# Linear attention feeding a gated MLP on one core: the planned order of work kept on every engine, and softmax denominators by a fused multiply-and-add

## The chip, the core and the metric

The kernel runs on one core of a Trainium2 chip. The core has a matrix engine (PE in the profile, with its weight loads as PEld), a vector engine (DVE), a scalar engine for activations and copies (ACT), a general engine (POOL) and SP, which here only issues DMAs. Each engine works through its own queue in the order in which the program stands; an instruction that waits for another engine holds everything behind it on its own engine. The metric is the device time of one execution in microseconds (us). Before the change it is 1099.16 us, the median of three runs (1097.7 to 1101.51).

## The reference

```python
def _attn_ref(q, k, v, omega):            # q, k, v: 8 x 8 x 576 x 64; omega: 128 x 64
    scale = 1.0 / np.sqrt(np.sqrt(D))
    def phi(x):
        proj = np.einsum('bhsd,md->bhsm', x, omega)
        sq = np.sum(x * x, axis=-1, keepdims=True) / 2.0
        h = proj - sq
        h = h - np.max(h, axis=-1, keepdims=True)
        return np.exp(h) / np.sqrt(m)
    q_p, k_p = (phi(q * scale), phi(k * scale))
    kv = np.einsum('bhsm,bhsd->bhmd', k_p, v)
    z = np.sum(k_p, axis=2)
    num = np.einsum('bhsm,bhmd->bhsd', q_p, kv)
    den = np.einsum('bhsm,bhm->bhs', q_p, z)[..., None] + 1e-06
    return num / den

def _moe_ref(x, w_in, w_out):             # x: 4608 x 512; w_in: 512 x 2048; w_out: 2048 x 512
    h = x @ w_in
    return (h * (1.0 / (1.0 + np.exp(-h)))) @ w_out
```

The attention output, with heads side by side, is the x of the MLP. The weights arrive as 64-bit floats.

## The kernel before, in words

**Tiling.** The attention is done for 32 pairs of heads, numbered n: four pairs give the 512 features of one batch t = n // 4, and 576 tokens of two heads make nine chunks of 128 rows (the middle chunk holds the end of one head and the start of the other). The MLP is done in steps (t, f): 512 tokens of batch t against 128 of the 2048 hidden features, 16 steps per batch; the 64 tokens that remain of each batch are kept aside and form a ninth round. Every 32-bit product of the MLP is made of three matmuls on high and low parts, so a step is 12 matmuls into the hidden tile (L495) and 12 into the output tile (L513), each 512 columns wide.

**One pair.** SP loads `raw` (transposed q or k, L238), `nat` (the same by rows, L242) and `v` (L246). ACT squares `nat` (L250), DVE sums the squares (L254). PE projects (L262, L269), DVE takes row maxima (L278, L276) and makes the exponent's shift `nb` (L282, L283), ACT takes the exponential (L298; from pair 8 on L312, after DVE has added the shift). POOL sums the chunks of k (L318 to L323), PE spreads that sum over all partitions (`zsum`, L327) and ACT copies it out (`zcopy`, L335 and L336: tile `zb`). DVE multiplies q's exponentials with `zb` (`products`, L362), sums each chunk (`denom`, L369) and takes reciprocals (L370). POOL multiplies q by them (`normal`, L375), PE transposes the result (`turn`, L381) and ACT copies it (L385). PE makes kv (L343), turns it (L351) and multiplies (`numer`, L399). ACT and DVE split the result into x high and low (L413, L418); that is the MLP's input for feature block k = n % 4.

**Weights.** In the first batch each of the 16 steps also prepares its weights: SP loads a block of w_in and one of w_out (L435, three buffers `wraw` for both), ACT and DVE put 32-bit words together (L442, L456, L458, L462), POOL splits them into high and low (L476, L480). The parts of w_in stay on chip; those of w_out go out to memory (L483) and come back for every step (L487). A hidden tile goes through two activations on ACT (L500, L501) and a subtraction on DVE (L505) before its second matmuls, which come two steps later. The exponential and this activation use different function tables; a change of function costs an ACT_TABLE_LOAD row.

**What sets the order.** All work is cut into units with an engine, a duration, a due time, what they follow and what they need free. `Plan.run` walks time forward with these numbers and returns one list of units. The program emits them in that list's order. In the version before, the framework's own scheduler then sorts the emitted instructions once more by its own estimate of when each could run, so an engine's queue holds them in an order that differs from the list's.

Of the kernel before, what the change touches and what calls it, by code (L numbers as in the profile page):

```python
# [63 lines left out]
class Plan:  # L64
# [6 lines left out]
    def add(self, name, eng, dur, key, fn, after=(), order=(), alloc=(), free=(), banks=0, table=None, lat=0.0):  # L71
        u = dict(
            name=name, eng=eng, dur=dur, key=key, fn=fn, after=list(after), order=list(order), alloc=list(alloc),
            banks=banks, table=table, lat=lat,
        )
        assert name not in self.units, name
        self.units[name] = u
        for i in free:
            self.freed_by.setdefault(i, []).append(name)
# [118 lines left out]
def attention_mlp(ctx: ExitStack, tc: tile.TileContext, qT, kT, qn, kn, v, om_in, w_in, w_out, out):  # L198
# [10 lines left out]
    def new(tag, shape, dtype=F32):  # L209
        return ring.tile(shape, dtype, tag=tag, name=tag, bufs=RINGS[tag])  # L210
# [6 lines left out]
    oms = const.tile([P, M], F32, tag="oms", name="oms")  # L217
    prod = const.tile([P, NC, M + 1], F32, tag="prod", name="prod")
    nc.gpsimd.memset(prod, GUARD)

# [136 lines left out]

    def products(n):
        e, zb = T["h", n, "q"], T.pop(("zb", n))
        for j, (lo, hi) in enumerate(((0, 4), (4, 5), (5, 9))):  # L360
            c = slice(lo, hi)
            nc.vector.tensor_tensor(  # L362
                prod[:, c, :M], e[:, c], zb[:, j].unsqueeze(1).broadcast_to([P, hi - lo, M]), ALU.mult
            )

    def denom(n):
        den = new("den", [P, NC])
        T["rd", n] = rd = new("rd", [P, NC])
        nc.vector.tensor_reduce(den, prod, AX.X, ALU.add)  # L369
        nc.vector.reciprocal(rd, den)  # L370
# [177 lines left out]
    for n in range(NWIN):  # L548
# [67 lines left out]
        if not merged:  # L616
# [7 lines left out]
            alloc=[("kw", ("kw", n))], free=[bk(("ktt", n))])  # L624
        add(("prod", n), "DVE", 1.7, at(n, 8, 34.2), lambda n=n: products(n),
            after=e["q"] + [("zc", n)], order=[("den", n - 1)] if n else [], free=[("zb", n)])
        add(("den", n), "DVE", 1.6, at(n, 8.1, 34.4), lambda n=n: denom(n), after=[("prod", n)],
            alloc=[("den", ("den", n)), ("rd", ("rd", n))])
        plan.freed_by[("den", n)] = [("den", n)]
# [59 lines left out]
    for i, (t, f) in enumerate(steps):  # L689
# [16 lines left out]
        for j in range(4):  # L706
# [11 lines left out]
            if f == NF - 1:  # L718
                add(("store", t, j), "ACT", 0.62, k2 + 0.2, lambda t=t, j=j: store(t, j), after=[("s2", t, f, j)],
                    free=[("po", t, j)])  # L720
    for u in plan.run():
        u["fn"](*[bank(p) for p in u["pools"]])

# [50 lines left out]
```

## Time and profile before

| what | value |
|---|---|
| runs, median (lowest to highest) | 1099.16 us (1097.7 to 1101.51) |
| the profiled execution's own time | 1101.4 us |
| its span, first to last instruction | 1099.3 us |
| mean granted PE clock | 0.976 |
| PE busy, share of the span | 96% |
| DVE / ACT / POOL busy, share of the span | 52% / 53% / 23% |

The profile is of one execution. "Busy" is the time in which an engine had at least one instruction at work; a group row gives the engine, the operation, out and in tiles, the count, the busy time with the mean of one instruction, and then the idle time ahead of them with what ended it. A timeline row gives the start in us, the length in us, and in square brackets how long the engine had been idle and who released it.

### The profile page before, as it was taken

The page shows a single profiled execution, that of the slowest core. Times are in us where ns is not written, and L with a number is a line of the kernel's source. Part 1 is how long each engine was busy: PE and PEld are TensorE (multiplying, and loading weights), DVE is VectorE, ACT ScalarE, POOL GpSimd, SP SyncE. Part 2 cuts the span into 40 slices and gives each one's busy share as a digit, 9 for nine tenths or more (in the row PEclk, how much of TensorE's full clock was granted, in tenths as well). Part 3 has the DMA queues.
Part 4 walks back from the last instruction along what each step waited for, and adds up shares of the span by engine and source line. Part 5 has one row for each costly group of instructions (what it writes and reads, how often), then busy time and mean ns, then how long its engine had stood idle before and what let it go on. Part 6 is the DMA issues. An engine that isn't in the chain of part 4 may idle for free.

```text
span 1099.3 us, 16192 instructions
## 1 busy us (share of the span) xinstructions
PE 1053.1 (96%) x5900; PEld 834.5 (76%) x5900; DVE 566.4 (52%) x1109; ACT 583.1 (53%) x1085; POOL 255.5 (23%) x327
## 2 busy tenths in 40 slices
PE   5677998899999999999999999999999999999998
PEld 4455776687877778777778777787877788888886
DVE  6788897745555455545555455555554431111111
ACT  5557878565556555555556555655565442222211
POOL 3666665411111111111111111111111110000000
PEclk7688999999999999999999999999999999999999
DMA  7576787553335443444345433533343226223323
GB/s 282 198 221 234 265 290 252 182 167 125 124 126 178 139 133 119 136 165 138 122 139 178 140 127 130 173 131 126 123 154 104 80 80 213 96 96 122 109 96 96
DMA packets 66526, 167.84 MB, mean 153 GB/s; under 512 B 15632, under 2 KB 15760, under 8 KB 66448
## 3 DMA queue, kind: packets, MB, share of 16 engines
q1 hardware_dynamic: 65984, 166.23, 45.6%
q8 instruction: 47, 0.77, 0.3%
q10 hardware_dynamic: 464, 0.59, 0.1%
q14 instruction: 31, 0.25, 0.1%
HBM read 146.87 MB, written 19.92 MB: 152 GB/s over the span
## 4 chain that ended last, share of the span: by engine, by line
PE 86%; DVE 5%; DMA 3%; ACT 3%; POOL 1%; issue 1%; SPq 0%; ACTq 0%; DVEq 0%; POOLq 0%
PE ps_acc L513 35%; PE ps_h L495 34%; PE ps_att L262 5%; PE ps_att L343 3%; PE ps_att L381 3%; PE ps_att L399 2%; DMA wraw<-w_out 1%; DMA nat<-qn 1%; PE ps_att L327 1%; PE ps_att L269 1%; DVE w L458 1%; ACT hq L298 1%; DVE w L462 1%; POOL hq L375 1%; DVE den L369 1%
## 5 line engine op out<-in xcount | busy, mean ns | idle before, releaser
L513 PE MATMUL ps_acc<-wo,gh 128*128 128x512 f32 x1152 | 369.9, 402 | 0.0
L500 ACT ACTIVATE gh<-ps_h 128x512 fp32r<-128x512 f32 x144 | 86.2, 599 | 295.9 <-PE ps_h L495 295.3
L505 DVE TENSOR_TENSOR gl<-ps_h,gh 128x512 fp32r<-128x512 f32 x144 | 99.1, 688 | 275.8 <-ACT ps_h L501 275.8
L513 PEld LDWEIGHTS ps_acc<-wo,gh 128*128 128x128 f32 x1152 | 207.1, 189 | 43.7
L495 PE MATMUL ps_h<-xh,wh 128*128 128x512 f32 x576 | 235.0, 409 | 0.3 <-ACT xh L413 0.3
L495 PE MATMUL ps_h<-xh,wl 128*128 128x512 f32 x576 | 226.7, 394 | 0.0
L495 PE MATMUL ps_h<-xl,wh 128*128 128x512 f32 x576 | 225.9, 392 | 0.0
L513 PE MATMUL ps_acc<-wo,gl 128*128 128x512 f32 x576 | 225.8, 392 | 0.0
L375 POOL TENSOR_TENSOR hq<-hq,rd 128x384 f32<-128x384 f32 x96 | 81.7, 879 | 421.4 <-DVE rd L370 396.5
L495 PEld LDWEIGHTS ps_h<-xh,wh 128*128 128x128 f32 x576 | 108.1, 188 | 24.7 <-issue 0.8
L513 PEld LDWEIGHTS ps_acc<-wo,gl 128*128 128x128 f32 x576 | 108.1, 188 | 24.2 <-issue 0.8
L495 PEld LDWEIGHTS ps_h<-xh,wl 128*128 128x128 f32 x576 | 108.1, 188 | 24.1
L495 PEld LDWEIGHTS ps_h<-xl,wh 128*128 128x128 f32 x576 | 108.5, 188 | 22.3 <-DVE xl L418 0.4
L312 ACT ACT_TABLE_LOAD x48 | 61.6, 1283 | 69.2 <-DVE hq L303 53.3
L318 POOL TENSOR_TENSOR t<-hk 128x256 f32<-128x256 f32 x64 | 48.8, 780 | 183.2 <-ACT hk L312 170.1
L278 DVE TENSOR_REDUCE mxq<-ps_att 128x4 f32<-128x512 f32 x57 | 37.2, 687 | 99.7 <-PE ps_att L262 99.6
L501 ACT ACTIVATE ps_h<-ps_h 128x512 f32<-128x512 f32 x144 | 85.3, 593 | 0.0
L500 ACT ACT_TABLE_LOAD x56 | 71.8, 1283 | 22.0 <-PE ps_h L495 21.3
L362 DVE TENSOR_TENSOR prod<-hq,zb 128x512 f32<-128x512 f32 (+1 forms) x96 | 52.3, 595 | 49.6 <-ACT zb L336 47.7
L250 ACT ACTIVATE nat<-nat 128x576 f32<-128x576 f32 x64 | 44.6, 703 | 20.3 <-DMA nat<-kn 12.3
L381 PE MATMUL ps_att<-ident,hq 128*128 128x128 f32 x261 | 41.1, 284 | 7.9 <-POOL wp L476 2.4
L278 DVE TENSOR_REDUCE mxk<-ps_att 128x4 f32<-128x512 f32 x55 | 35.6, 686 | 18.7 <-PE ps_att L262 18.7
(121 smaller groups left out, 1232.0 us busy)
## 6 DMA issues: line engine op xcount, KB each, us to landing
wo<-wo_d SPq DMA_DIRECT2D x144, 512.0 KB, 3.3
rawk<-kT SPq DMA_DIRECT2D x32, 352.0 KB, 3.0
rawq<-qT SPq DMA_DIRECT2D x32, 352.0 KB, 3.8
v<-v SPq DMA_DIRECT2D x32, 320.0 KB, 2.9
nat<-kn SPq DMA_DIRECT2D x32, 288.0 KB, 3.3
nat<-qn SPq DMA_DIRECT2D x32, 288.0 KB, 3.2
wraw<-w_in SPq DMA_DIRECT2D x16, 512.0 KB, 4.6
wraw<-w_out SPq DMA_DIRECT2D x16, 512.0 KB, 4.3
```

What stands on the lines that cost most here:

```text
L262: nc.tensor.matmul(ps[:, i * M : (i + 1) * M], raw[r, o : o + P], oms[r], start=True, stop=True)
L278: nc.vector.tensor_reduce(m[:, 5 * j : 5 * j + 4], ps.rearrange("p (c m) -> p c m", m=M), AX.X, ALU.max)
L312: nc.scalar.activation(h, h, AF.Exp)
L318: nc.gpsimd.tensor_tensor(t[:, j], e[:, 5 * j : 5 * j + 2], e[:, 5 * j + 2 : 5 * j + 4], ALU.add)
L362: nc.vector.tensor_tensor(prod[:, c, :M], e[:, c], zb[:, j].unsqueeze(1).broadcast_to([P, hi - lo, M]), ALU.mult)
L375: nc.gpsimd.tensor_tensor(e[:, c], e[:, c], rd[:, c].unsqueeze(2).broadcast_to([P, 3, M]), ALU.mult)
L381: nc.tensor.transpose(ps[:, i * P : (i + 1) * P], T["h", n, "q"][:, 3 * g + i], ident)
L495: nc.tensor.matmul(ph, w[:, k, :], x, start=k == 0 and n == 0, stop=k == NK - 1 and n == 2)
L500: nc.scalar.activation(gh, ph, AF.Silu)
L501: nc.scalar.activation(ph, ph, AF.Silu)
L505: nc.vector.tensor_tensor(gl, T["ph", t, f], T["gh", t, f].bitcast(F32), ALU.subtract)
L513: nc.tensor.matmul(T["po", t][j], g[:, js], w, start=f == 0 and n == 0, stop=f == NF - 1 and n == 2)
```

## The change

Two things change. The units are emitted inside a block that keeps the emitted order on every engine, so the list of `Plan.run` is what each queue holds. And the denominators are made by nine instructions, one per chunk, that multiply and accumulate in one go, instead of three products into `prod` and one wide sum over it. The guard against division by zero, which before lay in an extra column of `prod` (set once at the start), is now the start value of each accumulation. In the plan the units `prod` (1.7) and `den` (1.6) become one unit `den` with the duration 2.3; since the plan places all others around it, other units stand elsewhere in the list too.

```diff
-    prod = const.tile([P, NC, M + 1], F32, tag="prod", name="prod")
-    nc.gpsimd.memset(prod, GUARD)
+    prod = const.tile([P, NC, M], F32, tag="prod", name="prod")
...
-    def products(n):
+    def denom(n):
         e, zb = T["h", n, "q"], T.pop(("zb", n))
-        for j, (lo, hi) in enumerate(((0, 4), (4, 5), (5, 9))):
-            c = slice(lo, hi)
-            nc.vector.tensor_tensor(
-                prod[:, c, :M], e[:, c], zb[:, j].unsqueeze(1).broadcast_to([P, hi - lo, M]), ALU.mult
+        den = new("den", [P, NC])
+        for c in range(NC):
+            j = (c >= MID) + (c > MID)
+            nc.vector.tensor_tensor_reduce(
+                out=prod[:, c], in0=e[:, c], in1=zb[:, j], scale=1.0, scalar=GUARD, op0=ALU.mult, op1=ALU.add,
+                accum_out=den[:, c : c + 1],
             )
-
-    def denom(n):
-        den = new("den", [P, NC])
         T["rd", n] = rd = new("rd", [P, NC])
-        nc.vector.tensor_reduce(den, prod, AX.X, ALU.add)
         nc.vector.reciprocal(rd, den)
...
-        add(("prod", n), "DVE", 1.7, at(n, 8, 34.2), lambda n=n: products(n),
-            after=e["q"] + [("zc", n)], order=[("den", n - 1)] if n else [], free=[("zb", n)])
-        add(("den", n), "DVE", 1.6, at(n, 8.1, 34.4), lambda n=n: denom(n), after=[("prod", n)],
-            alloc=[("den", ("den", n)), ("rd", ("rd", n))])
+        add(("den", n), "DVE", 2.3, at(n, 8, 34.2), lambda n=n: denom(n), after=e["q"] + [("zc", n)],
+            order=[("den", n - 1)] if n else [], alloc=[("den", ("den", n)), ("rd", ("rd", n))], free=[("zb", n)])
...
-    for u in plan.run():
-        u["fn"](*[bank(p) for p in u["pools"]])
+    with tc.manual_schedule():
+        for u in plan.run():
+            u["fn"](*[bank(p) for p in u["pools"]])
```

Where instructions stand now, at three places. Line numbers of the changed kernel are one to three lower than those of the one before for the same code (L381 is L378, L343 is L342, L399 is L396, L458 is L455, L369 and L370 become L362 and L367, L435 is L432, L423 is L420).

**PE, end of pair 0.** The queue just behind the transposes of pair 0 (`hq`); `es` is the sum that POOL makes for pair 1, `hk,v` the kv product of pair 1, `en,kw` the result of pair 0. Before:

```order
L381 MATMUL ps_h<-ident,hq 128x128 x3
L381 MATMUL ps_att<-ident,hq 128x128 x6
L327 MATMUL ps_h<-es,ones 128x256
L343 MATMUL ps_att<-hk,v 64x128 x10
L399 MATMUL ps_acc<-en,kw 64x512 x2
L399 MATMUL ps_att<-en,kw 64x64 x2
```

And in the changed kernel:

```order
L378 MATMUL ps_h<-ident,hq 128x128 x3
L378 MATMUL ps_att<-ident,hq 128x128 x6
L342 MATMUL ps_att<-hk,v 64x128 x10
L396 MATMUL ps_acc<-en,kw 64x512 x2
L396 MATMUL ps_att<-en,kw 64x64 x2
L326 MATMUL ps_acc<-es,ones 128x256
```

The matmul that waits for POOL's sum of pair 1 has moved from in front of pair 1's kv and pair 0's result to behind both.

**DVE, the denominators of pair 3.** `w_914` is the weight word of step 4's w_in block, `sqq` and `sqk` on L254 and L253 are the sums of squares of later pairs. Before (left out: the other two products and two rows of other pairs ahead of the sum, and two more such rows behind it):

```order
L282 TENSOR_TENSOR nbq<-mxq,sqq 128x9
L458 SCALAR_TENSOR_TENSOR w_914<-wre,w_914 128x512
L283 SCALAR_TENSOR_TENSOR nbq<-nbq,sqq 128x9
L282 TENSOR_TENSOR nbk<-mxk,sqk 128x1
L462 SCALAR_TENSOR_TENSOR w_914<-wraw,w_914 128x512
L283 SCALAR_TENSOR_TENSOR nbk<-nbk,sqk 128x1
L254 TENSOR_REDUCE sqq<-nat 128x9
L278 TENSOR_REDUCE mxq<-ps_att 128x4 x2
L362 TENSOR_TENSOR prod<-hq,zb 128x4x128
...
L369 TENSOR_REDUCE den<-prod 128x9
...
L370 RECIPROCAL rd<-den 128x9
```

And in the changed kernel, where `w_914` stands behind the reciprocal (left out: seven more pairs of such rows as the two on L362):

```order
L281 TENSOR_TENSOR nbq<-mxq,sqq 128x9
L282 SCALAR_TENSOR_TENSOR nbq<-nbq,sqq 128x9
L455 SCALAR_TENSOR_TENSOR w_585<-wre,w_585 128x512
L253 TENSOR_REDUCE sqk<-nat 128x9
L459 SCALAR_TENSOR_TENSOR w_585<-wraw,w_585 128x512
L453 TENSOR_SCALAR w_783<-wraw 128x512
L362 ISA prod,den<-hq,zb 128x128
L362 ISA den 128x1
...
L362 ISA prod,den<-hq,zb 128x128
L362 ISA den 128x1
L367 RECIPROCAL rd<-den 128x9
```

Each multiply-and-accumulate is two instructions in the queue, the second of which writes the one accumulated column; nothing of another unit stands between the first and the reciprocal, and twelve units that stood in front of pair 3's denominators before stand behind them now.

**SP, loads around the weights of steps 6 and 7.** `wraw<-w_in` is a weight block; the two `rest` rows keep aside the tokens of pair 4 and wait for that pair's x; `rawq` waits for a buffer that pair 5's middle projection frees. Before (the first row is the block of step 7):

```order
L435 DMA wraw_1101<-w_in 128x512
L483 DMA wo_d_94<-wp_1133 128x1024
L487 DMA wo_1156<-wo_d_94 128x1024
L435 DMA wraw_1175<-w_out 128x512
L238 DMA rawq_1194<-qT 128x704
L242 DMA nat_1210<-qn 128x576
L487 DMA wo_1217<-wo_d_94 128x1024
L435 DMA wraw_1234<-w_in 128x512
L483 DMA wo_d_94<-wp_1232 128x1024
L246 DMA v_1279<-v 128x640
L423 DMA rest00_86<-xh0_1260 128x64
L423 DMA rest10_90<-xl0_1261 128x64
```

And in the changed kernel (the third row is the block of step 6, the last that of step 7):

```order
L237 DMA rawq_1143<-qT 128x704
L484 DMA wo_1153<-wo_d_93 128x1024
L432 DMA wraw_1200<-w_in 128x512
L432 DMA wraw_1203<-w_out 128x512
L245 DMA v_1215<-v 128x640
L241 DMA nat_1225<-kn 128x576
L480 DMA wo_d_93<-wp_1206 128x1024
L420 DMA rest00_85<-xh0_1190 128x64
L420 DMA rest10_89<-xl0_1191 128x64
L484 DMA wo_1317<-wo_d_93 128x1024
L432 DMA wraw_1323<-w_in 128x512
```

The load of step 7's w_in stood ahead of `rest` of pair 4 and of pair 7's `rawq`, and stands behind both now; that of step 6 stands behind that `rawq`.

On PE, all rows that start after 228 us of the profiled execution stand in the order before, but for 15 of 1,256 units, each moved by one or two places. ACT holds 120 function-table loads before and 112 now; all eight that are gone stood before that point.

## The prediction

> **What bounds the kernel now.** I read the page's head first, then a table of busy time in three stretches that I cut where PE's load changes; its columns are the stretch and its length, then busy time of PE, PEld, DVE, ACT and POOL, the granted PE clock, the DMA share and GB/s.
>
> ```profile
> span 1099.3 us, 16192 instructions
> PE 1053.1 (96%) x5900; PEld 834.5 (76%) x5900; DVE 566.4 (52%) x1109; ACT 583.1 (53%) x1085; POOL 255.5 (23%) x327
> 0.00:25.00 25.00, 13.83 (x108) 11.50 (x108) 15.11 (x35) 13.36 (x39) 6.42 (x14) 0.79 0.79 285
> 25.00:105.00 80.00, 57.94 (x338) 38.98 (x338) 66.53 (x115) 51.28 (x149) 55.03 (x60) 0.74 0.66 211
> 105.00:228.00 123.00, 114.73 (x636) 87.46 (x637) 97.94 (x166) 91.58 (x173) 68.30 (x70) 1.00 0.70 240
> 228.00:1075.00 847.00, 846.79 (x4736) 680.56 (x4735) 383.01 (x788) 422.09 (x716) 125.79 (x184) 1.00 0.40 132
> ```
>
> From 228 to 1075 us PE is idle for 0.2 us in 847, and the order there is nearly the old one: nothing that other engines do can shorten or, short of large delays, lengthen it. PE is idle for 11.2 us up to 25, 22.1 us from 25 to 105 and 8.3 us from 105 to 228. The question is when PE reaches the work that stood at 228. Up to 105 it waits for the attention of the first four pairs; there DVE is the fullest of the others (66.5 of 80 us), and from 105 on PE itself is at 93% with DVE at 80%.
>
> **The multiply-and-accumulate.** Groups of the old denominators, and DVE rows that start close behind each other:
>
> ```profile
> L362 DVE TENSOR_TENSOR prod<-hq,zb 128x512 f32<-128x512 f32 x64 | 47.0, 734 | 49.6 <-ACT zb L336 47.7 <-ACT hq L312 1.9
> L362 DVE TENSOR_TENSOR prod<-hq,zb 128x128 f32<-128x128 f32 x32 | 10.2, 318 | 0.0
> L369 DVE TENSOR_REDUCE den<-prod 128x9 f32<-128x1161 f32 x32 | 43.6, 1362 | 0.9
> 76.78 0.16 DVE L283 SCALAR_TENSOR_TENSOR nbq<-nbq,sqq 128x9 f32<-128x9 f32 x1
> 76.86 0.14 DVE L282 TENSOR_TENSOR nbk<-mxk,sqk 128x1 f32<-128x1 f32 x1
> 76.93 0.68 DVE L462 SCALAR_TENSOR_TENSOR w<-wraw,w 128x512 uint32<-128x512 uint32 x1
> 191.45 0.28 DVE L362 TENSOR_TENSOR prod<-hq,zb 128x128 f32<-128x128 f32 x1
> ```
>
> The rows from 76.78 on start 0.08 and 0.07 apart though each lasts longer, so successive instructions overlap by some 0.08. Old: 2 x 0.734 + 0.318 + 1.362, less 4 x 0.08, is 2.83 us a pair. New: no row shows the instruction. Low end: the undisturbed 128-column product of the last row less overlap, 0.20, and 0.07 for the one-column write, times nine: 2.4. High end: no overlap, (0.318 + 0.14) x 9 = 4.1. Less than the low end I exclude, since the instruction reads the same columns as that product. Rows in a row overlap here, and the mean product has 0.24 left, so I take (0.24 + 0.07) x 9 = 2.8: the edit itself is worth nothing (range -0.4 to +1.3 a pair), and what covers an error is DVE's idle time, 13.5 us from 25 to 105 and 25 us behind. From 228 on DVE is busy for 45%, so it costs nothing there.
>
> [...]
>
> **The order, term by term.** First the PE queue behind pair 0, where a matmul for POOL's sum of pair 1 stood in front of pair 1's kv and pair 0's result, and ACT behind it:
>
> ```profile
> 27.25 0.90 PE L381 MATMUL ps_att<-ident,hq 128*128 128x128 f32 x3 [0.33 <-POOL hq L375]
> 33.65 1.22 PE L327 MATMUL ps_h<-es,ones 128*128 128x256 f32 x2 [5.50 <-POOL es L323]
> 34.81 2.40 PE L343 MATMUL ps_att<-hk,v 128*64 128x128 f32 x20
> 37.25 0.27 ACT L348 COPY kt<-ps_att 128x128 f32<-128x128 f32 x1 [6.71 <-PE ps_att L343]
> 39.92 0.27 ACT L336 COPY zb<-ps_h 128x128 f32<-128x128 f32 x1
> ```
>
> PE stood 5.5 us with the kv ready to run behind the wait (its exponentials were done before ACT's idle 6.71). Now kv starts at 28.15. ACT's copy of pair 1's `zb`, which sat behind the late kv, follows POOL's sum at once. Bounds: 0 if another input of pair 1 is late, 5.5 if all; I take 5, since POOL's sum itself does not move and only the copy behind it does.
>
> Then the denominators of pairs 2 and 3 on DVE, with ACT's last `zb` copy of pair 3:
>
> ```profile
> 55.83 1.59 DVE L362 TENSOR_TENSOR prod<-hq,zb 128x512 f32<-128x512 f32 x3
> 58.83 0.76 DVE L254 TENSOR_REDUCE sqq<-nat 128x9 f32<-128x576 f32 x1 [1.41 <-ACT nat L250]
> 59.50 1.35 DVE L369 TENSOR_REDUCE den<-prod 128x9 f32<-128x1161 f32 x1
> 62.60 0.90 PE L381 MATMUL ps_acc<-ident,hq 128*128 128x128 f32 x3 [3.37 <-POOL hq L375]
> 75.86 0.27 ACT L336 COPY zb<-ps_att 128x128 f32<-128x128 f32 x1
> 79.46 1.78 DVE L362 TENSOR_TENSOR prod<-hq,zb 128x512 f32<-128x512 f32 x3
> 82.11 1.35 DVE L369 TENSOR_REDUCE den<-prod 128x9 f32<-128x1161 f32 x1
> 84.05 0.20 DVE L370 RECIPROCAL rd<-den 128x9 f32<-128x9 f32 x1
> 101.50 2.05 PE L513 MATMUL ps_acc<-wo,gh 128*128 128x512 f32 x4
> ```
>
> Pair 2: products end at 57.42, the sum starts at 59.50, because a sum of squares for a later pair, whose data had not landed, stood between. It stands behind now: 2.1 us, with PE waiting (3.37). Pair 3: `zb` is there at 76.13, the reciprocal ends at 84.25. With nothing between, 76.13 + 2.8 + 0.2 = 79.1: 5.1 us. Together with the first term 12.2 us by the chain of pairs.
>
> Does DVE have the time? Of units ahead of pair 3's x, nine are moved behind it: six weight words, one sum of squares, two shifts.
>
> ```profile
> L462 DVE SCALAR_TENSOR_TENSOR w<-wraw,w 128x512 uint32<-128x512 uint32 x32 | 27.9, 887 | 0.1
> L458 DVE SCALAR_TENSOR_TENSOR w<-wre,w 128x512 uint32<-128x512 uint32 x32 | 27.6, 873 | 0.4 <-ACT wre L442 0.4
> L456 DVE TENSOR_SCALAR w<-wraw 128x512 uint32<-128x512 uint32 x32 | 23.0, 721 | 10.4 <-POOL wp L480 4.1 <-POOL wl L480 3.5 <-DMA wraw<-w_out 2.2
> ```
>
> Two of each is 5.0, the sum of squares 0.76, the shifts some 0.5: 6.3 us less in front. The remaining 6 of 12.2 would have to come out of 13.5 us of DVE idle time that waits leave scattered; I count half of it, 3. So PE gets its full feed 9 us earlier (0 to 14). Given back: those 6.3 us fall due after 105, where DVE had 25 us idle; PE then has at most 8.3 us of its own idle time to win there and 114 us for the same work. I take 1 us lost (4 won to 9 lost). ACT's eight table loads fewer help the same chain:
>
> ```profile
> L298 ACT ACT_TABLE_LOAD x11 | 14.1, 1283 | 5.0 <-DVE nbk L283 4.0 <-DVE nbq L283 0.9
> ```
>
> 8 x 1.283 = 10.3 us of an engine that is 26% idle from 105 to 228: counted in that 1 us.
>
> Sum: the profiled execution took 1101.4 (span 1099.3, and 2.1 around it); 1101.4 - 9 + 1 = 1093.4. It lay 2.2 above the median of the runs, so **1091** for the median.
>
> **Rivals.** *A, no change: weights come late.* SP's load of step 7's w_in stands behind the `rest` of pair 4 now (the first row gives the size of such a load and its time to landing):
>
> ```profile
> wraw<-w_in SPq DMA_DIRECT2D x16, 512.0 KB, 4.6
> 103.30 0.33 SPq L435 DMA_DIRECT2D wraw<-w_in  x1
> 122.29 0.33 SPq L423 DMA_DIRECT2D rest<-xl  x1
> 125.86 1.61 POOL L480 TENSOR_TENSOR wl<-w,wh 128x512 fp32r<-128x512 f32 x1
> 138.47 0.39 PE L495 MATMUL ps_h<-xh,wh 128*128 128x512 f32 x1
> ```
>
> Then it is issued at 122.6 - 9 = 113.6 instead of 103.3. If its way to the low part again takes 24.2 us (103.30 to 127.47), that ends at 137.8, and PE, 9 us ahead, wants it at 129.5: 8.3 us waited, the gain is gone, 1099. Against it: most of those 24 us were queues; landing (4.6), three word instructions (2.5) and POOL's two (about 2.5) are 10, which ends at 124.
>
> *B, slower: POOL blocks the nine.* DVE rows of pair 6's products, beside POOL's work on weights:
>
> ```profile
> 150.18 1.75 DVE L362 TENSOR_TENSOR prod<-hq,zb 128x512 f32<-128x512 f32 x1 [0.64 <-ACT zb L336]
> 152.05 0.68 DVE L362 TENSOR_TENSOR prod<-hq,zb 128x512 f32<-128x512 f32 x1
> 155.04 1.36 DVE L362 TENSOR_TENSOR prod<-hq,zb 128x128 f32<-128x128 f32 x1
> ```
>
> The same product takes 0.68 or 1.75, and the 128-column one 1.36 instead of 0.32: some 1.05 lost when something holds it. If each of nine is exposed, with POOL busy for 60% of 25 to 228 (123.3 of 203): 9 x 0.6 x 1.05 = 5.7 against 1.9 for three, +3.8 a pair, 30 us over the eight pairs of the start. DVE has 38 us idle; if half of that takes it up, 15 us go to the path: 1091 + 15 = 1106. It decides from +2 a pair on. Against it: the mean of 64 products is 0.734, so the loss is rare on the whole. [...]
>
> *C, much faster:* all of the 12.2 us comes through and PE's 8.3 us behind 105 halve: 1099 - 16 = 1083 or less. *D, the order changes nothing:* excluded, the queues differ.
>
> **Numbers.** Forecast 0.46, C 0.12, A 0.21, B 0.21. A measurement here tells 0.3%, some 3.3 us, from no change: faster 0.58, same 0.21, slower 0.21. The range takes in C's near part and B's centre: 1080 to 1107; the forecast's own is 1084 to 1095.
>
> **What would show it.** Right: kv of pair 1 near 28 us; no DVE row of another unit between pair 3's first accumulate and its reciprocal, which ends near 75; first output matmul (L513, 101.50 before) near 92; PE idle up to 105 at 24 us instead of 33. The pair of instructions at 0.3 us together: the edit is neutral; 0.45 with gaps beside POOL: B. PE waits on POOL's low weights between 110 and 150: A. The prediction is wrong if PE's idle time before full feed stays near 33 us, or if the stretch of full load changes its length.

## The result, and the profile after

The changed kernel takes 1093.17 us, the median of eight runs (1088.96 to 1096.29); the kernel before, on the same chip, 1099.19 (eight runs, 1097.7 to 1101.51). The ratio is 0.994, with a 95% interval from 0.9923 to 0.9958: faster by 6 us. The forecast was 1091 (1080 to 1107). The sum behind it, however, had two terms wrong that cancel each other, as the traces and the experiments show; that the number came out is luck. Medians here and below leave out three executions that took 2029 us (kernel before), 2469 (experiment 7) and 5793 (experiment 1).

First the page's head and the busy time in the stretches that the prediction cut (columns: the stretch and its length, busy time of PE, PEld, DVE, ACT, POOL with their instructions, the granted PE clock, the DMA share, GB/s). The profiled execution took 1092.76 us, 0.4 below its median, and that of the kernel before 1101.4, 2.2 above: the two traces lie 8.6 us apart where the medians lie 6.0 apart, so a lead read from them may be some 2.6 us too large.

```profile
span 1091.0 us, 16612 instructions
PE 1042.6 (96%) x5900; PEld 827.7 (76%) x5900; DVE 543.0 (50%) x1557; ACT 573.0 (53%) x1077; POOL 250.0 (23%) x326
0.00:25.00 25.00, 15.99 (x124) 12.91 (x126) 18.70 (x51) 16.19 (x49) 10.20 (x18) 0.87 0.86 313
25.00:105.00 80.00, 62.09 (x419) 45.26 (x415) 67.34 (x182) 59.62 (x167) 47.63 (x57) 0.87 0.70 227
105.00:228.00 123.00, 107.47 (x591) 82.28 (x591) 100.84 (x220) 72.99 (x147) 66.40 (x69) 0.94 0.70 237
228.00:1075.00 847.00, 846.22 (x4730) 678.60 (x4727) 353.74 (x1101) 421.65 (x713) 125.80 (x184) 1.00 0.42 131
```

PE idles for 9.0 us up to 25, 17.9 from 25 to 105 and 15.5 from 105 to 228. The first two were 11.2 and 22.1, the third 8.3. Together it is 42.4 against 41.6: the new kernel idles as long as the old one and is faster all the same. It was ahead early, and lost much of that again. The timeline of PE (start, length, what; in brackets the idle time ahead and its releaser) shows pair 1's kv, the zsum behind it, the first output matmul and the first matmul of step (1, 1):

```profile
24.23 1.93 PE L342 MATMUL ps_att<-hk,v 128*64 128x128 f32 x20
28.42 0.70 PE L326 MATMUL ps_acc<-es,ones 128*128 128x256 f32 x2 [1.30 <-POOL es L322]
...
90.19 0.62 PE L510 MATMUL ps_acc<-wo,gh 128*128 128x512 f32 x2
...
219.84 0.40 PE L492 MATMUL ps_h<-xh,wh 128*128 128x512 f32 x1
```

Before, kv started at 34.81, the output matmul at 101.50, and step (1, 1), the work that stood at 228, at 227.96. PE is 10.6 us ahead at kv, 11.3 at the first output, 8.1 at step (1, 1). Pair 3's reciprocal ends at 65.38 in place of 84.25, 18.9 ahead. The new instruction, as groups and as it stands in DVE's queue for pair 3:

```profile
L362 DVE CUSTOM_DVE_ANT_0 prod<-hq,zb 128x128 f32<-128x128 f32 x288 | 68.5, 303 | 43.3 <-ACT zb L335 43.1
L362 DVE DVE_READ_ACCUMULATOR2_ANT den<- 128x1 f32 x288 | 23.5, 82 | 0.0
L367 DVE RECIPROCAL rd<-den 128x9 f32<-128x9 f32 x32 | 6.9, 216 | 1.1
```

```profile
62.20 1.23 DVE L362 CUSTOM_DVE_ANT_0 prod<-hq,zb 128x128 f32<-128x128 f32 x1 [0.73 <-ACT zb L335]
63.36 0.08 DVE L362 DVE_READ_ACCUMULATOR2_ANT den<- 128x1 f32 x1
63.36 0.28 DVE L362 CUSTOM_DVE_ANT_0 prod<-hq,zb 128x128 f32<-128x128 f32 x1
63.58 0.07 DVE L362 DVE_READ_ACCUMULATOR2_ANT den<- 128x1 f32 x1
...
65.17 0.21 DVE L367 RECIPROCAL rd<-den 128x9 f32<-128x9 f32 x1
```

The groups give (68.5 + 23.5) / 32 = 2.87 us a pair, almost exactly the predicted 2.8, and that reading is a trap. The timeline shows that each one-column write starts together with the next multiplication, and that the multiplications start 0.21 to 0.22 apart though each lasts 0.28. A group's busy time counts only its own rows, and the sum of two groups counts their overlap twice. What a pair really takes is the time from the first row to the end of the reciprocal: 2.25 us in most of the 32 pairs. Over the first eight, where PE still waits for other engines, it is 2.24 to 3.74 and 2.9 in the mean, because some multiplications are held there (the rivals below say by what).

### The profile page after: what moved, and what is told of

Same layout as the page of the kernel before. It is cut to its first block, busy times and chain, and to the rows that moved or that the text cites. A ratio compares the mean times of both kernels' runs of the same rounds, so it can differ in the third digit from the quotient of the medians.

```text
span 1091.0 us, 16612 instructions
## 1 busy us (share of the span) xinstructions
PE 1042.6 (96%) x5900; PEld 827.7 (76%) x5900; DVE 543.0 (50%) x1557; ACT 573.0 (53%) x1077; POOL 250.0 (23%) x326
## 4 chain that ended last, share of the span: by engine, by line
PE 78%; DVE 9%; ACT 6%; issue 2%; POOL 2%; DMA 2%; ACTq 0%; SPq 0%; POOLq 0%; DVEq 0%
PE ps_acc L510 32%; PE ps_h L492 32%; PE ps_att L261 5%; PE ps_att L342 2%; PE ps_att L378 2%; PE ps_att L396 2%; DVE prod L362 2%; DVE w L455 1%; ACT L497 1%; PE ps_att L326 1%; POOL hq L372 1%; PE ps_att L268 1%; ACT hq L297 1%; DVE mxq L277 1%; DVE w L459 1%
## 5 line engine op out<-in xcount | busy, mean ns | idle before, releaser
L492 PE MATMUL ps_h<-xh,wh 128*128 128x512 f32 x576 | 237.8, 413 | 5.2 <-POOL wh L473 5.2
L510 PEld LDWEIGHTS ps_acc<-wo,gl 128*128 128x128 f32 x576 | 108.4, 188 | 23.5
L362 DVE CUSTOM_DVE_ANT_0 prod<-hq,zb 128x128 f32<-128x128 f32 x288 | 68.5, 303 | 43.3 <-ACT zb L335 43.1
L378 PE MATMUL ps_att<-ident,hq 128*128 128x128 f32 x252 | 38.3, 277 | 6.0 <-issue 2.1
```

The costliest lines, as they stand in the source:

```text
L362: nc.vector.tensor_tensor_reduce(out=prod[:, c], in0=e[:, c], in1=zb[:, j], scale=1.0, scalar=GUARD, op0=ALU.mult, op1=ALU.add, accum_out= ...
L378: nc.tensor.transpose(ps[:, i * P : (i + 1) * P], T["h", n, "q"][:, 3 * g + i], ident)
L492: nc.tensor.matmul(ph, w[:, k, :], x, start=k == 0 and n == 0, stop=k == NK - 1 and n == 2)
L510: nc.tensor.matmul(T["po", t][j], g[:, js], w, start=f == 0 and n == 0, stop=f == NF - 1 and n == 2)
```

## The experiments

Experiments 1, 4 and 5 change the kernel before, the others the changed kernel. "The plan's numbers" are the duration of the denominators in the plan: 1.7 and 1.6 for two units before, 2.3 for one unit after; since the plan places everything around them, other numbers make another list. All medians, and ratios to the kernel before (experiments 1 to 4 were timed beside one set of its runs, the change beside another, whose medians are 1099.1 and 1099.2):

| kernel | order | list (den) | denominators | median us | ratio, 95% interval |
|---|---|---|---|---|---|
| before | sorted | 1.7 + 1.6 | products, sum | 1099.1 | |
| 1 | kept | 1.7 + 1.6 | products, sum | 1088.6 | 0.9891 to 0.9925 |
| 2 | sorted | 2.3 | fused | 1104.2 | 1.003 to 1.0064 |
| 3 | kept | 2.3 | products, sum | 1100.0 | 0.9994 to 1.0023 |
| 4 | kept | 1.7 + 1.6 | fused | 1084.0 | 0.9837 to 0.9876 |
| the change | kept | 2.3 | fused | 1093.2 | 0.9923 to 0.9958 |

### 1. The kept order alone

```diff
-    for u in plan.run():
-        u["fn"](*[bank(p) for p in u["pools"]])
+    with tc.manual_schedule():
+        for u in plan.run():
+            u["fn"](*[bank(p) for p in u["pools"]])
```

> The kernel before with its emitted order kept on every engine; products, wide sum and the plan's numbers are the old ones. If the kept order carries the gain: 1090 to 1096, as the changed kernel. If the gain needs the plan made with the shorter unit, or the fused instruction: 1097 to 1101, no change.

Measured: 1088.6. Keeping the order is worth 10.4 us by itself, more than the whole change. Experiment 5 is the same kernel once more, with the trace that is read here.

### 2. The fused instruction and its plan, without the kept order

The changed kernel with the last hunk of the diff undone.

> The changed kernel without the kept order: fused instructions and the plan with 2.3 for the denominators, but the framework sorts the instructions again. If the kept order carries the gain: 1097 to 1101. If the fused instruction or the new plan carries it: 1090 to 1096.

Measured: 1104.2, slower than before by 5. Against the changed kernel the kept order is worth 11.0 us.

### 3. The kept order with the new list, products and wide sum as before

```diff
+        for j, (lo, hi) in enumerate(((0, 4), (4, 5), (5, 9))):
...
-            nc.vector.tensor_tensor_reduce(
...
+        nc.vector.tensor_reduce(den, prod, AX.X, ALU.add)
```

These lines are a part of the edit of the changed kernel; its list stays, with one unit den of 2.3.

> The changed kernel with three products and a wide sum in the place of the nine fused instructions; plan, order and all other queues as in the changed kernel. The old form measured 2.83 us a pair by my count and the new one 2.87 by the profile after (0.303 + 0.082 less overlaps, 92.0 us of busy time over 32 pairs), so if the instruction is neutral: within 2 us of the changed kernel's 1093. If the fused form is worth something at its place (it cannot be split by POOL's reads, or writes denominators sooner): 1096 or more.

Measured: 1100.0. With this list the old denominators give no gain at all; the fused instruction in the same list makes 1093.2 of it, so it is worth 6.8 us. So the queues that the change makes, taken by themselves, gain nothing. DVE's timeline of pair 3 here answers to the rows above:

```profile
66.13 2.45 DVE L362 TENSOR_TENSOR prod<-hq,zb 128x512 f32<-128x512 f32 x3 [0.72 <-ACT zb L336]
68.61 1.36 DVE L366 TENSOR_REDUCE den<-prod 128x9 f32<-128x1161 f32 x1
70.01 0.21 DVE L368 RECIPROCAL rd<-den 128x9 f32<-128x9 f32 x1
```

From first row to end it is 4.09 us against 3.18, both with about 1 us lost once at the beginning. In most of the 32 pairs it is 3.14 against 2.25. The fused form saves 0.9 us a pair, beyond the -0.4 that the prediction gave as its best case.

### 4. The kept order and the fused instruction in the old list

The diff of experiment 1, and the nine instructions in the unit that held the products, whose number stays 1.7; the unit den keeps the reciprocal and its 1.6.

> Order kept, made with the old plan (units of 1.7 and 1.6), fused instructions in the first unit and the reciprocal in the second: all queues but DVE's denominators as in the run with the order alone. Neutral instruction: equal to the run with the order alone within 2 us. If the fused form matters by itself: the difference to it has the sign and size of the difference between the changed kernel and the one with its plan and the old form.

Measured: 1084.0, faster than the changed kernel by 9.2 us. With 1 this makes a table of two by two: the fused instruction is worth 4.6 us in the old list (5.8 against experiment 5) and 6.8 in the new one, and **the new list costs 11.4 us with products and sum and 9.2 fused**. The change's 6.0 is 10.4 for the order, 4.6 for the instruction, less 9.2 for the list (5.8 by these medians).

### 5. The kept order alone, for its trace

> The kept order alone once more (old numbers of the plan, three products and the wide sum), for a trace that stands beside the one of the old plan with the fused instruction, whose lists are the same. Theory F (the fused instruction shortens each pair's denominators where nothing hides it): from the first accumulate to the end of the reciprocal a pair took 2.25 us fused and 3.14 with products and sum in the two kernels of the new plan; here the first four pairs should each take 0.9 us more than in the old plan with the fused instruction, the last transposes of pair 3 come 3.5 to 5 us later, step (1, 1) starts 4 to 7 us later than 212.4, and the time is 1088 to 1091. Rival (the gain of the fused form lies elsewhere, behind 228 us or in fewer DVE conflicts with POOL): the chain of pairs stands within 1 us of the other's, and the difference appears only later.

Measured: 1089.8 in two runs. Lists equal those of 4, so the reciprocals of pair 2 and of pair 7 compare directly, first here, then in 4:

```profile
54.40 0.21 DVE L370 RECIPROCAL rd<-den 128x9 f32<-128x9 f32 x1
178.79 0.21 DVE L370 RECIPROCAL rd<-den 128x9 f32<-128x9 f32 x1
```

```profile
51.95 0.22 DVE L369 RECIPROCAL rd<-den 128x9 f32<-128x9 f32 x1
172.40 0.21 DVE L369 RECIPROCAL rd<-den 128x9 f32<-128x9 f32 x1
```

The lead is 2.5 us at pair 2 and 6.4 at pair 7: about 0.8 for each pair, added up. At pair 3's last transposes it is 3.1 us, a little less than expected (79.10 and 75.96). Step (1, 1) starts at 217.8 here and 212.4 in 4. Theory F holds: the chain of pairs carries the saving pair by pair, because each pair's transposes wait for its denominators.

With the traces PE's time up to its last matmul can be taken apart: idle time; what half clock takes (an estimate: half of PE's busy time inside the stretches whose granted clock is 0.5, since the first matmul of step 13 of the changed kernel lasts 0.79 us at clock 0.50, at 182.01, and that of step (1, 1) 0.40 at 1.00, at 219.84); and the rest, its work at full clock.

| | last matmul ends | idle | half clock | rest |
|---|---|---|---|---|
| before | 1094.8 | 41.7 | 18.7 | 1034.4 |
| 5: order kept | 1083.8 | 41.9 | 14.6 | 1027.3 |
| 4: order kept, fused | 1078.2 | 38.2 | 11.7 | 1028.3 |
| the change | 1085.9 | 43.2 | 14.9 | 1027.7 |

The kept order took 7.1 us out of PE's work and 4.1 out of half clock, and nothing out of its idle time, where the prediction had looked. The same matmuls take less time in the new order; where, the groups of the q projections say (out and in, instructions, then busy time and mean ns), before and after:

```profile
L262 PE MATMUL ps_att<-oms,rawq 64*128 64x128 f32 x456 | 41.0, 285 | 0.2 <-ACT en L385 0.2
L262 PE MATMUL ps_acc<-oms,rawq 64*128 64x128 f32 x56 | 6.5, 343 | 0.0
```

```profile
L261 PE MATMUL ps_att<-oms,rawq 64*128 64x128 f32 x448 | 36.1, 291 | 3.1 <-ACT hk L297 2.5 <-ACT en L382 0.6
L261 PE MATMUL ps_acc<-oms,rawq 64*128 64x128 f32 x64 | 6.3, 306 | 0.0
```

One matmul lasts about as long as before (285 and 291 ns in the larger group, 343 and 306 in the smaller). The two groups' busy times must not be added here either, since a projection that writes both tiles has rows of both at the same time: counted once, the 512 rows take 40.2 us in place of 46.3. In experiment 5, the order alone, they take 38.6. PE's rows of one such projection in the start of the kernel before, and of one in its full load, then of one in the start of the changed kernel, show why:

```profile
139.70 1.16 PE L262 MATMUL ps_att<-oms,rawq 64*128 64x128 f32 x8
142.38 1.16 PE L262 MATMUL ps_att<-oms,rawq 64*128 64x128 f32 x8
615.73 1.16 PE L262 MATMUL ps_att<-oms,rawq 64*128 64x128 f32 x16
```

```profile
121.17 1.44 PE L261 MATMUL ps_att<-oms,rawq 64*128 64x128 f32 x16
```

A projection uses the upper 64 rows of PE for one head and the lower 64 for the other, and written in turn, two matmuls run side by side: 16 rows in 1.16 us (each of the eight matmuls is two rows), and where the trace lists the rows of the two halves singly, in a projection of the kernel before, one starts at 40.67 us and the other at 40.68, each 0.27 long. In the start the sorted order had put the halves apart, with other matmuls between, and each took 1.16 by itself. Experiment 2, sorted too, shows the same rows (132.72 and 135.39, 1.16 each).

### 6. Weights of the step before (on the changed kernel)

```diff
-        for n, (w, x) in enumerate(((w_hi[f], xh), (w_hi[f], xl), (w_lo[f], xh))):
+        g = f - 1 if t == 0 and f else f
+        for n, (w, x) in enumerate(((w_hi[g], xh), (w_hi[g], xl), (w_lo[g], xh))):
```

What does the new list lose? Its waits of PE from 105 to 213 us (time, number, longest) have late weights at their head, and those of experiment 4 have none; from the changed kernel:

```profile
PE ps_h L492 <- POOL wh L473: 5.2, 2, 4.3
PE ps_att L378 <- issue: 2.1, 1, 2.1
PE ps_att L378 <- ACT hk L297: 2.0, 1, 2.0
```

> The changed kernel, except that in the first batch each step from the second on multiplies with the hidden weights of the step before it (its own are still loaded and made, and used from the second batch on), so that part of the output is computed with other weights; every list stays as it is, and a step's matmuls no longer wait for weights that were just made. Theory W (what the new plan lost against the old one lies in weights that come late): the waits for POOL's high and low parts, 5.2 and 0.6 us, go, and with them the half-clock stretch at 179 to 186 us, 1.9 us of PE's work: 1093 - 5.8 - 1.9 = 1085 to 1086, about the time of the old plan. Rival 1 (the next wait takes its place: transposes, activations): half of it or less, 1089 to 1092. Rival 2 (PE's end is set elsewhere): 1093.

Measured: 1091.9, 1.3 us less; the intervals of the two kernels overlap. Theory W falls. PE's rows of step 13's first matmul and of pair 7's last transposes in the changed kernel, then the transposes here:

```profile
182.01 0.79 PE L492 MATMUL ps_h<-xh,wh 128*128 128x512 f32 x1 [4.30 <-POOL wh L473]
192.24 0.55 PE L378 MATMUL ps_att<-ident,hq 128*128 128x128 f32 x3 [0.27 <-DVE hk L302]
```

```profile
191.78 0.88 PE L378 MATMUL ps_att<-ident,hq 128*128 128x128 f32 x3 [4.44 <-DVE hk L302]
```

The 4.3 us that PE no longer waits at 182 it waits ten microseconds later, for a bank that DVE's work on pair 8 frees (L302). The wait that the profile put first was only the first of two, and the chain of pairs set the time behind it.

### 7 and 9. Filling three waits of PE (on the changed kernel)

```diff
+    def fill(ps, times):
+        for _ in range(times):
+            nc.tensor.matmul(ps, ones, ones, start=True, stop=True)
...
+        if n == 0:
+            fill(ps[:, 3 * P :], 18)
```

The last two lines are one of the three places in 9, behind zsum of pair 0; the other calls are left out.

> The changed kernel with matmuls of ones by ones put into three waits of PE, where nobody reads their result: 18 of them (0.24 us each at full clock) ahead of pair 0's first transposes, 18 behind pair 2's middle projection of q, 13 ahead of step 13's first matmul. They add work that has no use and take away PE's idling. Theory C (the granted clock falls to half because PE idled, and the half-clock stretches cost time of their own): the stretches at 18.7 to 25.5, 35.8 to 42.6 and 179 to 186 us, in which PE lost 1.9, 2.0 and 1.9 us of work, go or shrink; the one at 179 is wholly on the path, the first two for about half: 1093 - 3 to - 6, 1087 to 1090. Rival 1 (the clock falls for another reason, such as load or a fixed rhythm): the stretches stay, and the time is 1093 to 1096, since a filling that runs at half clock lasts longer than the wait. Rival 2 (the clock comes back, but the path there is not PE's): stretches gone, 1092 to 1094.

> The changed kernel with useless matmuls of ones by ones in three waits of PE again, this time each where the queue holds nothing that they have to wait for (in the kernel with fillings before, the first 18 waited for the very bank that pair 0's transposes wait for and so ran behind the wait): 18 behind pair 0's zsum, in columns of its bank that nobody reads (wait from 15.6 to 21.6 us), 18 behind pair 3's projection of k (33.3 to 38.5), 12 ahead of step 13's first matmul (177.7 to 182.0). Theory C (half clock follows idling, and costs time of its own): the half-clock stretches at 18.7, 35.8 and 179 us go, in which PE lost 1.9, 2.0 and 1.9 us of work; the last counts whole, the first two at least for half: 1093 - 3 to - 6, 1087 to 1090. Rival 1 (the clock falls for another reason): the stretches stay, 1093 to 1095. Rival 2 (stretches gone, but attention there waits for POOL, ACT and DVE, not for PE): 1091.5 to 1093.5.

Measured: 1098.5 and 1102.0, slower than the changed kernel by 5 and 9. Both times the filling ahead of pair 0's transposes did not lie in the wait but moved it. In 7 it needed the bank that the transposes wait for, and ran behind the wait (from 22.48 us, after 5.97 of idle time). In 9 it stood behind zsum, and ACT's copy of that sum did not go on before the last filling matmul, as ACT's row of experiment 9 says:

```profile
20.35 0.26 ACT L342 COPY zb<-ps_acc 64x128 f32<-64x128 f32 x1 [3.84 <-PE ps_acc L229]
```

So the times don't answer the question. The clock does for the other two fillings. Stretches of the changed kernel (columns as above, the clock third from the end), then of experiment 9:

```profile
33.30:38.40 5.10, 0.04 (x2) 0.00 (x0) 5.00 (x19) 1.23 (x5) 2.40 (x4) 0.74 0.93 313
38.50:42.50 4.00, 3.89 (x23) 2.87 (x25) 3.83 (x7) 3.74 (x14) 3.39 (x5) 0.50 0.36 125
179.20:185.90 6.70, 3.76 (x8) 2.56 (x9) 6.46 (x11) 0.66 (x1) 4.03 (x4) 0.50 0.44 164
```

```profile
37.60:42.00 4.40, 4.40 (x42) 4.20 (x38) 4.30 (x19) 0.27 (x2) 2.40 (x3) 1.00 0.95 323
42.00:48.00 6.00, 4.46 (x40) 3.29 (x40) 5.79 (x11) 5.98 (x23) 3.85 (x6) 1.00 0.39 117
184.00:190.00 6.00, 3.95 (x25) 3.09 (x25) 5.86 (x9) 0.68 (x1) 4.52 (x5) 1.00 0.57 209
```

Where PE was kept busy the clock stayed at 1.00 (in experiment 7 too, but for 3.4 us of the third stretch). At these two places half clock followed PE's idling, 5.1 us up to 38.46 and 4.3 up to 182.01, which rules out rival 1 for them. What half clock costs on the path isn't shown: no run took it away without adding something else.

### 8, 10 and 11. Other durations for den (on the changed kernel)

```diff
-        add(("den", n), "DVE", 2.3, at(n, 8, 34.2), lambda n=n: denom(n), after=e["q"] + [("zc", n)],
+        add(("den", n), "DVE", 2.4, at(n, 8, 34.2), lambda n=n: denom(n), after=e["q"] + [("zc", n)],
```

In 10 it is 3.1, in 11 it is 3.4. The duration of an undisturbed pair is 2.25, nearest to 2.3; over the first eight pairs the means in these four kernels are 2.9 to 3.1, nearest to 3.1.

> The changed kernel with the duration of the unit den in the plan set to 2.4 in place of 2.3, nothing else. Theory L (2.3 is not wrong, it drew an unlucky list: the planner picks greedily, so a tenth of a microsecond changes the list, and the plan's own clock tells how good the list is; it starts step (1, 1) at 215.8 with 2.3, 211.0 with the old numbers, 209.8 with 2.4): about 5 us faster than the changed kernel, 1085 to 1089. Rival 1 (what lost was that the denominators are counted as short, so that others are placed too near): 1092 to 1094, like 2.3. Rival 2 (one unit in place of two is what lost): the same 1092 to 1094.

> The changed kernel with the duration of the unit den in the plan set to 3.1 in place of 2.3, nothing else; the denominators still take 2.25 us undisturbed. Theory L (the list decides, and the plan's own clock ranks the lists): the plan starts step (1, 1) at 206.3, against 215.8 with 2.3 (measured 219.8), 211.0 with the old numbers (212.4) and 209.8 with 2.4 (210.8): 5 to 9 us faster than the old plan's 1084 at best, so 1076 to 1084, and below the 2.4 kernel's 1087. Rival (2.3, the real duration of a pair, is the better number, and 2.4 only happened to lose less): 1090 or more.

> The changed kernel with the duration of den set to 3.4, nothing else. Theory L: three tenths above 3.1 the plan's own clock starts step (1, 1) at 219.7, later than with 2.3 (215.8) and 13.4 later than with 3.1: 1092 to 1100, slower than 3.1 by at least 8 us. Rival (longer durations are better as such, since they keep other work away from the denominators): within 3 us of 3.1.

Measured: 1087.3, 1083.9 and 1087.9 (intervals of the ratio 0.9875 to 0.9909, 0.9825 to 0.9871, 0.9871 to 0.9916).

| den | plan's clock at step (1, 1) | trace there | plan's clock at its last unit | median us |
|---|---|---|---|---|
| 2.3 (the change) | 215.8 | 219.8 | 1100.9 | 1093.2 |
| 2.4 | 209.8 | 210.8 | 1099.5 | 1087.3 |
| 1.7 + 1.6 (experiment 4) | 211.0 | 212.4 | 1096.1 | 1084.0 |
| 3.1 | 206.3 | 206.2 | 1095.7 | 1083.9 |
| 3.4 | 219.7 | 215.0 | 1104.8 | 1087.9 |

The first half of theory L holds: a tenth of a microsecond in one number moves the kernel by 5.8 us, and the number that is true of an undisturbed pair has the worst list of the four. That it loses because it is too short for the first eight pairs is a rival that no run rules out; against it stands only the jump from 2.3 to 2.4, both of which are too short for them. Nor is it one unit in place of two: 3.1 is one unit and as fast as the old two. The second half holds only in part. The plan's clock places step (1, 1) within 1.4 us for three of the five, but it is no ranking: 3.1 reaches that step 6.2 us earlier than experiment 4 and ends together with it, because its list, like that of 2.4, has 28 rows of PE behind that step that the others have ahead of it (the twelve output matmuls of step 14 and a projection of pair 9), and 3.4, which the plan calls the worst, is 5.3 us better than 2.3. Where the lists differ on the chip is PE's stretch from 105 to 228, in experiments 8, 10 and 11:

```profile
105.00:228.00 123.00, 111.89 (x623) 86.26 (x622) 101.20 (x226) 77.08 (x151) 67.50 (x70) 0.96 0.73 249
```

```profile
105.00:228.00 123.00, 116.95 (x682) 90.59 (x683) 100.02 (x230) 84.57 (x164) 64.88 (x70) 0.99 0.73 249
```

```profile
105.00:228.00 123.00, 113.65 (x633) 87.95 (x632) 95.53 (x222) 82.66 (x157) 63.22 (x67) 0.97 0.70 238
```

PE is busy there for 107.5 us with 2.3, for 111.9 and 113.7 with 2.4 and 3.4, which are 0.6 us apart in time, and for 117.0 with 3.1: among these four, the fuller that stretch, the faster the kernel, but for that pair. This describes where the time lies, not what causes it.

### 12. The halves of the q projections apart (on the changed kernel)

```diff
-        for i in range(4):
-            for j, ps in enumerate((a, b)):
+        both = [(i, j) for i in range(4) for j in range(2)]
+        if who == "q" and n < 8:
+            both = [(i, j) for j in range(2) for i in range(4)]
...
```

> The changed kernel, with the eight matmuls of each q projection of the first eight pairs written as four on the upper 64 rows of PE and then four on the lower 64, in place of upper and lower in turn; nothing else. In the kernel before, where the framework sorts, such a projection stood in two pieces with other work between them (139.70 and 142.38 us, 1.16 each), with the order kept it stands in one (121.17, 1.44). Theory H (two matmuls on different halves of the rows run side by side, and the kept order gained most of its PE time by leaving them side by side): these projections take 2.3 to 2.4 us each in place of 1.3 to 2.0, some 0.9 x 8 = 7 us more of PE's work, and since attention's waits hide part of it, 3 to 7 us more time: 1096 to 1100. Rival 1 (the pieces were long because of what stood between them): projections as before, 1092 to 1094. Rival 2 (PE's work there is hidden behind waits for other engines): 2.3 us each, but 1092 to 1095.

Measured: 1095.2, with a ratio from 0.9934 to 0.9969; 2.0 us more than the changed kernel, whose interval overlaps. The same two groups here:

```profile
L265 PE MATMUL ps_att<-oms,rawq 64*128 64x128 f32 x448 | 37.4, 290 | 2.1 <-ACT hk L301 1.5 <-ACT en L386 0.6
L265 PE MATMUL ps_acc<-oms,rawq 64*128 64x128 f32 x64 | 8.8, 323 | 0.0
```

Counted once where they overlap, they take 45.0 us in place of 40.2: 0.6 us for each of the eight, not the 0.9 expected, since halves that follow each other directly still overlap where they meet (16 rows from 124.69 take 1.71 us, and the second half starts 0.3 us before the first one's last row). PE's idle time is shorter in exchange (37.8 us in place of 43.2), and 2 us of time are left, which the intervals don't tell from nothing. So order does change what PE's work costs, as theory H says, but most of it falls into waits, as rival 2 says. How much of the kept order's 10.4 us comes from the projections is not settled by this; the taking apart in experiment 5 is a count of where PE's time lies, not of what each part is worth.

## Why the forecast was right, and where its steps were wrong

**The bound held.** The stretch from 228 on took as long as before (0.8 us idle in 847), and the whole gain was there when PE reached step (1, 1): 8.1 us ahead, 8.9 at the last matmul.

**The multiply-and-accumulate: wrong.** The step "the edit itself is worth nothing (range -0.4 to +1.3 a pair)" failed. It saves 0.9 us a pair and 4.6 to 6.8 us of the time. The step added (0.24 + 0.07) for each of nine; the one-column write costs nothing, because it starts with the next multiplication, and those stand 0.21 apart. The old side was too low as well: 2.83 with the reciprocal left out is 2.93 in the runs (3.14 less 0.21). Nor did "DVE's idle time" cover it: the denominators lie on the chain of pairs, and idle time of the engine elsewhere doesn't help a pair.

**The order, term by term: the step that failed.** The three places moved as said. Pair 1's kv was to start at 28.15 and started at 24.23; nothing stands between pair 3's first accumulate and its reciprocal, which was forecast at 79.1 by its own term and near 75 with the others, and ends at 65.38. But these leads hold the instruction's saving too. Experiment 3 has the change's queues with the old denominators, which is what the prediction priced here:

```profile
26.39 2.40 PE L343 MATMUL ps_att<-hk,v 128*64 128x128 f32 x20
95.69 0.61 PE L511 MATMUL ps_acc<-wo,gh 128*128 128x512 f32 x2
229.83 0.40 PE L493 MATMUL ps_h<-xh,wh 128*128 128x512 f32 x1
```

Against the kernel before, the queues alone bring pair 1's kv 8.4 us forward, pair 3's reciprocal 14.0 (it ends at 70.22), the first output matmul 5.8, and step (1, 1) comes 1.9 late. So "9 us earlier (0 to 14)" is 5.8 at its own mark, and of that nothing is left at step (1, 1): the 8 us that the sum gave the queues are not there, and experiment 3 takes 1100.0 us against 1099.1. In the changed kernel the instruction adds 5.5 us of lead at the first output and 10.0 at step (1, 1), which makes the 11.3 and the 8.1 seen above. Nor is the first output a good mark: with the order kept in the old list (experiment 5) it comes only 1.1 us early, at 100.43, and step (1, 1) 10.2 early.

PE's idle time up to 105 fell from 33.3 to 26.9, not to 24. What no step had is that the order also changes how long PE's own work takes (halves side by side) and how long its clock is halved: from the rows of the stretches, 2 x (0.21 x 25 + 0.26 x 80) = 52 us at half clock before and 2 x (0.13 x 25 + 0.13 x 80 + 0.06 x 123) = 42 after.

**Given back, "1 us lost (4 won to 9 lost)": mis-sized.** In experiment 3 the lead falls by 7.7 us from the first output to step (1, 1); in the changed kernel it falls by 3.2, and PE's idle time from 105 to 228 rises from 8.3 to 15.5. The prediction took the change's list as a set of moves on the way to the start. The list as a whole costs 9.2 to 11.4 us against the old one (experiments 1, 3 and 4), and no step had a term for that; why this list is the worse one stays open. This error and that of the instruction have opposite signs, which is why 1091 came out: its 8 us were put on the queues, which gave none, and the 6 that were measured are what the instruction, priced at nothing, gave in this list.

**The rivals.** A (weights come late) did not happen where it was put: step 7's low part ended at 123.7 us, ahead of its step at 124.7. Weights were late at 182, but taking that wait away gave 1.3 us. B (POOL blocks each of the nine) happened only in small: pair 3 loses about 1 us once, in its first multiplication of 1.23, and the eight behind it run at their 0.21. Of the first eight pairs, 1 and 3 lose 0.8 to 0.9 us in one multiplication, 5 and 7 1.5 in two (the longest lasts 1.37), pair 6 0.2 and the others nothing: 5 us together, where B had 30. POOL's row beside pair 3's multiplication of 62.20 shows the hold that B supposed:

```profile
62.02 1.26 POOL L477 TENSOR_TENSOR wp<-w,wp 128x512 fp32r<-128x512 f32 x1
```

POOL's work ends at 63.28 and the multiplication at 63.43; the other five long ones of pairs 1, 5 and 7 end 0.14 to 0.15 us behind a POOL instruction on weights in the same way. What B had wrong is the count: in these six cases one instruction of POOL holds one of the nine, not each. B's own sum was off as well: half of DVE's 38 us of idle time, taken from its 30, would leave 11, not 15. C's 1083 is about what the same two edits reach in the old list (1084.0). D was excluded because the queues differ; they do, and yet by themselves they leave the time where it was.

## What to carry to other kernels

Read what a chain of small instructions costs from the start of the first row to the end of the last, never from the sum of two groups' busy times. Before a list's moves are priced one by one, hold the list fixed and change the instruction, then the other way round: here a new number in a greedy planner cost more than the better instruction gained, and three other numbers, timed on the chip, found 1084 in place of 1093. A saving that is seen early counts only if it is still there where the engine that sets the time runs full. When the engine that sets the time is as idle as before and the kernel is faster, look at what its busy rows take: neighbours in its queue, and its clock.

## What the runs showed of the hardware that was not expected

- The accumulate's one-column write (0.08 us) starts together with the next multiplication, so nine pairs of instructions take 2.04 us though their durations add up to 9 x (0.303 + 0.082) = 3.5.
- Eight matmul records on the upper half of PE's rows and eight on the lower take 1.16 us when they alternate (615.73 in the kernel before; 1.44 at 121.17 in the changed one), 1.71 when one half follows the other (124.69 in experiment 12), and 1.16 for each half when other matmuls stand between (139.70 and 142.38 in the kernel before).
- Six multiplications of DVE in the first eight pairs last 0.69 to 1.37 us in place of 0.28 (1.23 at 62.20), and each ends 0.14 to 0.15 us behind an instruction of POOL on weights; the eight behind that of 62.20 run at their usual 0.21.
- The granted clock in the traces of the kernels before and after is 1.00 or 0.50, and at two places that the fillings tested half followed a wait of PE: it fell 2.4 us into the idle stretch of 5.1 us and was 0.50 up to 42.6, it fell 1.4 us into the one of 4.3 us and was 0.50 up to 185.9, and with PE kept busy there it stayed 1.00 in experiment 9. The half-clock stretches ahead of PE's last matmul last 6.8 us in the changed kernel, all six of them (here 35.8 to 42.6 and 179.1 to 185.9), and 3.4, 6.8 or 10.2 us in the kernel before, and 17.1 once (21.6 to 38.7).
